# Linear attention's K^T V regrouped as (x^T K)^T Wv in a kernel with a searched instruction order

## The chip, the cores and the metric

The kernel runs on one core of a Trainium2 chip. A core has five engines that run their own instruction streams and meet at semaphores: TensorE (PE; its weight loads are shown as PEld), VectorE (DVE), ScalarE (ACT), GpSimd (POOL) and SyncE (SP), which here only issues transfers (DMAs). TensorE writes to PSUM, which DVE and ACT read; GpSimd works on SBUF alone. The metric is the time of one execution in microseconds of device time. Before the change it is 661.53 us (median of three runs, 661.41 to 661.91).

## The reference

Two attention blocks, A and B, each with an input x of 2048 rows by 512 columns in bf16, a weight wqkv of 512 by 1536 and a weight wo of 512 by 512. Both have 32 heads of 16. The outputs stand side by side, 2048 by 1024.

```python
# A: linear attention
phi = lambda t: jnp.where(t > 0, t + 1, jnp.exp(t)) + 1e-6
pq, pk = phi(q), phi(k)
kv = jnp.einsum("bhsd,bhse->bhde", pk, v)
z = jnp.einsum("bhsd->bhd", pk)
num = jnp.einsum("bhqd,bhde->bhqe", pq, kv)
den = jnp.einsum("bhqd,bhd->bhq", pq, z)[..., None] + 1e-6
o = num / den            # then o @ wo
# B: softmax attention
scores = jnp.einsum("bhqd,bhkd->bhqk", q, k) * scale
p = softmax(scores, axis=-1)
o = jnp.einsum("bhqk,bhkd->bhqd", p, v)      # then o @ wo
```

q, k and v are thirds of x @ wqkv, cut into heads.

## The kernel before

**B** is most of the work. Scores are computed transposed, in blocks of 128 keys by 512 queries, one head each: 32 heads, 16 key tiles and 4 query chunks make 2048 blocks. They are grouped into 32 units (`unit`): a group of 8 heads, a query chunk, and the even or the odd heads of the group, so that a unit has 64 blocks in four row groups of TensorE. `qk` computes a block; PV products add P times V (with a column of ones for the denominator) into `pPV`, one row group of heads to each 32 columns of TensorE.

The exponential of a block takes one of two ways:

- ACT (`fill_act_cand`): two or three blocks in `pS`, one exponential over 1024 or 1536 columns into `PT`, then one PV product for each block.
- The VectorE path (`fill_d_cand`, `d_pick`, `d_emit`): a block in a bank of `pD`, or in the third bank of `pS` (the planner's slot X), which DVE converts to an int16 that read as f16 approximates the exponential (line 980); two copies of it with other offsets, made by POOL (`on_pool`, line 1170) or by DVE (`on_dve`, line 1135); and three PV products, the first with V scaled (`VX`), the others with V (`VV`).

**A** is done in small jobs between the blocks. Each job takes one bank (`DBANK`: two of `pD` and slot X), issues its matmuls in stages and keeps the bank until a last stage has read it (`rel`). Before the change the jobs of A are, in this order:

- For each half `hp` of the 512 columns: `ak_job` and `av_job`, each eight times, for two row tiles at a time. `akv_mm` multiplies x transposed (`xTa`, loaded in chunks of 512 rows by a transposing DMA, two chunks in the buffer) by 256 columns of Wk or Wv. `ak_job` applies phi (ACT's exponential on line 686, two DVE steps on lines 687 and 689) into `KNa`; `av_job` copies to `VNa` (DVE, line 729), whose rows of 129 have a one at their end.
- `akvsum_job`, twice for each half: 16 matmuls of `KNa` tiles with 129 columns of `VNa` (line 736), then two DVE steps that mask the head blocks into `RHA` (lines 738 and 739).
- For each query chunk: `aq_job` four times (phi(q) into `PQT`), `aden_job`, and for each row tile `anum_job` and `aout_job`, the output projection and its store. `VNa` and `KNa` serve again there as `OA`, `ONT` and store buffers.

Only the first job of A's list may start, so A's jobs keep their order. Job i is not due before 40 + 560 i / N us by the planner's clock, N being the number of A's jobs: 88 before.

**The order** of every instruction on every engine is fixed when the kernel is built. A planner (the `while True` loop) keeps a clock for each engine, takes the candidate that can start first, breaks ties by priorities, and books it with a cost written in the code. A table `SEG` holds, for each stretch of the plan, 25 parameters of these choices: how many blocks go to the VectorE path at most (`RMX`, `DBL`, `PBL`), how full a batch of PV products must be (`PVQ`, `PVO`), when a shift goes to DVE (`PSH`, `DSH`), how many banks jobs may hold (`JM`), priorities, and noise with a seed (`NZ`, `SD`). The table was found by a search. Where the plan leaves PE idle, `fill_in` books products with zeros.

SP's queue issues nearly all transfers, in the order of the plan, and an issue that has to wait holds up those behind it: the loads at the start, A's x transposes (line 462), the 96 small copies that spread B's K over row groups (line 617), A's output transposes (line 795) and the stores (line 806).

Of the kernel before, what the change touches and what calls it, by code (L numbers as in the profile page):

```python
# [238 lines left out]
def bass_concat_heads__linear_attn_block__softmax_full_mha__prompt_kernel(nc, A_x, A_wqkv, A_wo, B_x, B_wqkv, B_wo, out):  # L239
# [11 lines left out]
    JM = 2  # L251
# [21 lines left out]
    DBL = 2.5  # L273
    PBL = 7.0
    SEG = (
# [66 lines left out]
    XAL = 7.0  # L342
    NZ = 0
# [16 lines left out]
    with es:  # L360
# [24 lines left out]
        VNa = sb("VNa", [128, NT, 2, 129], BF)  # L385
        PQT = sb("PQT", [128, 1, 4, 512], BF)
# [33 lines left out]
        def f32v(bk, n=512):  # L420
            return bk[0][:, bk[2]:bk[2] + n]
# [43 lines left out]
        load(Wa[:], wav, ["WaQ", "WaK"])  # L465
        wo_lane = sch.new_dma_lane()
# [48 lines left out]
        sch.add("pool", lambda e: e.memset(VNa[:, :, :, 128:129], 1.0), writes=["VNa1"])  # L515
# [177 lines left out]
        xa_left = [4] * 12  # L693
# [33 lines left out]
        def av_job(t2, hp, **kw):  # L727
            st = akv_mm(t2, hp, 2)
            st.append(("dve", 0.6, f_ev("dve", lambda e, bk: e.tensor_copy(VNa[:, t2:t2 + 2, :, 0:128], f32v(bk).rearrange("p (a b n) -> p a b n", a=2, b=2)),
                                        [], [("VNa", t2), ("VNa", t2 + 1)])))  # L730
            return Job(st, [("xA", 4 * hp + t2 // 4)] + ([("akv", hp - 1, bl) for bl in range(2)] if hp else []), [(2, ("av", hp, t2))], **kw)
# [705 lines left out]
        for hp in range(2):  # L1437
            for t in range(0, NT, 2):
                ajobs += [ak_job(t, hp), av_job(t, hp)]
# [235 lines left out]
```

## Time and profile before

| | |
|---|---|
| median of three runs | 661.53 us (661.41 to 661.91) |
| the profiled execution | 661.61 us |
| its span, first to last instruction | 659.9 us |
| granted TensorE clock, mean | 0.998 |
| score blocks in all | 2048 |
| shifts on DVE, on POOL (instructions) | 113, 369 |
| transfers on SP's queue: x transposes of A, K spreads, stores | 12, 96, 31 |
| HBM read, written | 4.46 MB, 4.19 MB |

How to read the lines that follow. A group is named by line, engine, operation and tiles, output first, with the shape of each; after the count stand the busy time, the mean duration in ns, and the idle time of the engine just before such instructions with what ended it. `x575` is the number of instructions. Instructions of one engine can overlap by a pipeline's depth, so starts can be closer than durations; matmuls do so most, and the busy time of PE counts a matmul until its modelled end. The chain of waits goes back from the last instruction to whatever released each step.

### The profile page before, as it was taken

The numbers are of one execution on the slowest core, as the hardware profiler recorded it, in microseconds if no ns is written. First come the engines' busy times: TensorE is split into PE (matmuls) and PEld (weight loads), VectorE is DVE, ScalarE is ACT, GpSimd is POOL, SyncE is SP. The second block draws the span as 40 slices with busy tenths as digits, with TensorE's granted clock in tenths as the row PEclk, the third lists the DMA queues.
The fourth block names the chain that finished last, engine by engine and source line by source line (L and its number), as shares of the span: only waits on it lengthen the run. The fifth ranks groups of instructions, "written<-read, shape, count | busy, mean of one in ns | idle before, by whom it ended". The sixth has DMA issues, their size and how long they took to land.

```text
span 659.9 us, 15950 instructions
## 1 busy us (share of the span) xinstructions
PE 633.2 (96%) x6609; PEld 200.4 (30%) x6662; DVE 632.0 (96%) x1089; ACT 644.7 (98%) x686; POOL 592.9 (90%) x450
## 2 busy tenths in 40 slices
PE   8999999999999999999999999999999999999996
PEld 5323333222333333332222233322222223232222
DVE  4999999999999999999999999999999999999994
ACT  6999999999999999999999999999999999999994
POOL 5999999999999999999998899999999999999982
PEclk9999999999999999999999999999999999999999
DMA  9701010020102101210012011010021000120002
GB/s 176 208 3 33 1 34 6 11 43 9 34 2 33 26 9 33 65 34 9 9 30 62 17 34 34 23 15 9 6 26 42 16 1 11 25 26 32 26 26 68
DMA packets 53214, 21.54 MB, mean 33 GB/s; under 512 B 44176, under 2 KB 52624, under 8 KB 53136
## 3 DMA queue, kind: packets, MB, share of 16 engines
q1 hardware_dynamic: 51664, 19.80, 13.9%
q8 instruction: 54, 0.88, 0.6%
q10 hardware_dynamic: 1472, 0.66, 0.4%
q14 instruction: 24, 0.20, 0.1%
HBM read 4.46 MB, written 4.19 MB: 13 GB/s over the span
## 4 chain that ended last, share of the span: by engine, by line
ACT 95%; PE 3%; DMA 1%; issue 0%; DVE 0%; DVEq 0%
ACT PT L1077 93%; ACT EA L686 2%; DMA xTb<-in_B_x_dram 1%; PE pPV L1247 1%; PE pD L802 1%; PE pS L864 0%; PE pD L1299 0%; PE pS L1299 0%; PE pS L1383 0%; DVE KNa L575 0%; PE pD L1383 0%; PE pD L652 0%; PE pD L864 0%; DVEq L1619 0%
## 5 line engine op out<-in xcount | busy, mean ns | idle before, releaser
L1077 ACT ACTIVATE PT<-pS 128x1024 f16<-128x1024 f32 (+1 forms) x648 | 636.6, 1305 | 1.0 <-PE pS L864 1.0
L1170 POOL TENSOR_SCALAR DI<-DI 128x2048 int16<-128x2048 int16 (+1 forms) x369 | 554.5, 1503 | 47.0 <-DVE DI L980 19.4
L980 DVE TENSOR_SCALAR DI<-pD 128x512 int16<-128x512 f32 x492 | 324.5, 679 | 6.1 <-PE pD L864 2.5
L864 PE MATMUL pS<-QT,KM 32*128 32x512 bf16 x1556 | 255.0, 384 | 8.6 <-ACT PT L1077 4.8
L1247 PE MATMUL pPV<-PT,VV 128*17 128x512 f16 x1369 | 233.7, 381 | 0.0
L1247 PE MATMUL pPV<-DI,VV 128*17 128x512 f16 x1358 | 227.3, 382 | 0.0
L864 PE MATMUL pD<-QT,KM 32*128 32x512 bf16 x492 | 170.6, 384 | 0.3 <-DVE PQT L689 0.3
L1247 PE MATMUL pPV<-DI,VX 128*17 128x512 f16 x679 | 161.0, 381 | 0.2 <-DVE OT L1276 0.2
L864 PEld LDWEIGHTS pS<-QT,KM 32*128 32x128 bf16 x1556 | 64.6, 91 | 264.8 <-ACT PT L1077 227.0
L980 DVE TENSOR_SCALAR DI<-pS 128x512 int16<-128x512 f32 x187 | 126.7, 677 | 0.7
L1135 DVE TENSOR_SCALAR DI<-DI 128x1056 int16<-128x1056 int16 x113 | 77.0, 687 | 0.5
L1247 PEld LDWEIGHTS pPV<-PT,VV 128*17 128x17 bf16 x1369 | 47.5, 88 | 41.4 <-issue 36.1
L1247 PEld LDWEIGHTS pPV<-DI,VV 128*17 128x17 bf16 x1358 | 47.0, 88 | 40.4 <-issue 33.0
L864 PEld LDWEIGHTS pD<-QT,KM 32*128 32x128 bf16 x492 | 40.6, 90 | 5.4 <-DVE DI L980 2.0
L1247 PEld LDWEIGHTS pPV<-DI,VX 128*17 128x17 bf16 x679 | 34.2, 88 | 22.0 <-issue 17.7
L711 PE MATMUL pD<-Wa,xTa 128*128 128x256 bf16 x200 | 30.5, 275 | 0.3 <-DVE DI L980 0.2
L593 PE MATMUL pD<-xTb,Wb 128*128 128x512 bf16 x67 | 21.2, 383 | 3.2 <-issue 2.3
L1276 DVE STREAM_TRANSPOSE OT<-pPV 128x512 f32<-128x512 f32 x31 | 21.9, 705 | 0.0
L575 DVE CAST KNa<-pD 128x512 bf16<-128x512 f32 x27 | 18.4, 681 | 3.0 <-PE pD L802 2.0
L1282 POOL TENSOR_TENSOR OT<-OT,ZR 128x256 bf16<-128x256 f32 x31 | 19.3, 622 | 1.6
L711 PEld LDWEIGHTS pD<-Wa,xTa 128*128 128x128 bf16 x200 | 15.5, 97 | 13.3 <-issue 6.3
L686 ACT ACTIVATE EA<-pD 128x512 bf16<-128x512 f32 x23 | 19.2, 834 | 0.0
(136 smaller groups left out, 346.0 us busy)
## 6 DMA issues: line engine op xcount, KB each, us to landing
out_dram<-KNa SPq DMA_DIRECT2D x31, 128.0 KB, 1.7
Wa<-in_A_wqkv_dram SPq DMA_DIRECT2D x1, 1536.0 KB, 7.8
KM<-KR SPq DMA_DIRECT2D x96, 16.0 KB, 1.8
Wb<-in_B_wqkv_dram SPq DMA_DIRECT2D x2, 384.0 KB, 4.3
Wb<-in_B_wqkv_dram SPq DMA_DIRECT2D x1, 512.0 KB, 5.0
Wa<-in_A_wo_dram SPq DMA_DIRECT2D x1, 512.0 KB, 4.2
Wa<-in_B_wo_dram SPq DMA_DIRECT2D x1, 512.0 KB, 4.2
ON<-in_B_x_dram ACTq DMA_DIRECT2D x1, 256.0 KB, 2.8
```

What stands on the lines that cost most here:

```text
L575: return lambda e, bk: (e.tensor_copy(out_fn(), in_fn(bk)) if lane == "dve" else e.activation(out_fn(), in_fn(bk), ACTF.Copy))
L593: return e.matmul(f32v(bk), lhsT=Wb[:, cc, kind * 512 + Gp * 128:kind * 512 + Gp * 128 + 128], rhs=xTb[:, cc, sc * 512:(sc + 1) * 512], st ...
L686: ("act", 0.052 + n * 0.000833, f_ev("act", lambda e, bk: e.activation(EA[:, 0:n], f32v(bk)[:, c0:c0 + n], ACTF.Exp), [], ["EA"])),
L711: return e.matmul(f32v(bk)[:, 256 * tt:256 * tt + 256], lhsT=xTa[:, b, cc, (o + tt) * 128:(o + tt + 1) * 128], rhs=Wa[:, cc, 512 * kind + ...
L864: return e.matmul(dst, lhsT=KM[32 * g:32 * g + 32, Gp % 2, e_, j * 128:(j + 1) * 128], rhs=QT[32 * g:32 * g + 32, Gp % 2, c * 512:(c + 1) ...
L980: sch.add("dve", lambda e: e.tensor_scalar(DI[:, buf, D0_ + i * 512:D0_ + (i + n) * 512], f32v(DBANK[b0], n * 512), ESC, EB, op0=ALU.mult, ...
L1077: sch.add("act", lambda e: e.activation(PTf[:, p0 * 512:p0 * 512 + w], S5[:, c0:c0 + w], ACTF.Exp, scale=SC), reads=skeys(sl, len(bl)), wr ...
L1135: sch.add("dve", lambda e: e.tensor_scalar(gapped(DI[:, buf, :], DIV[v], wide // 32, 32), DI[:, buf, D0_ - 32:D0_ + w], 1.0, float(SHIFT[v ...
L1170: sch.add("pool", lambda e: e.tensor_scalar(dv, sv, 1.0, sh_, op0=ALU.mult, op1=ALU.add), reads=keys, writes=[("DI", v_, x) for x, v_ in s ...
L1247: sch.add("pe", lambda e, g=g, j=j, c0=c0, V_=V_, r2=r2, P=P, first=first, last_=last_: e.matmul(PVb[32 * g:32 * g + 17, 0:512] if len(P.s ...
L1276: sch.add("dve", lambda e: e.transpose(OT[:, 0, :], PVb[:, 0:512]), reads=[("PV", g) for g in range(4)], writes=[("OT", 0)])
L1282: ("pool", 0.7, f_op("pool", lambda e: e.tensor_tensor(xn[:, :, 16 * e_:16 * e_ + 16], o[:, :, 0:16], zr.unsqueeze(2).broadcast_to([128, 1 ...
```

## The change

By the rule of matrix products phi(K)^T (x Wv) = (x^T phi(K))^T Wv. `av_job` and the projection of V are taken out. A new `axk_job` (two for each half `hp`, one for each half h of x's columns) computes x^T phi(K): 32 matmuls of 256 columns in eight stages, with x as the stationary operand in the layout it has in memory, 128 rows to a tile, and the result copied by DVE to a section of `PQT`. x's columns are loaded 256 at a time into `VNa`'s buffer, seen flat as `VNf`: the first half when the kernel starts, the second after the first `axk_job`, and the first again after the third. `akvsum_job` then has 16 matmuls of 8 columns with ones, for z, and 4 of 128 columns with Wv. `aq_job` of the first chunk waits for these sums, because `PQT` is shared. A has 76 jobs in place of 88. Chunks of x transposed are let go after two stage ends in place of four. Three base values differ (`JM`, `DBL`, and `XNL`, the planner's time for the new load) and the whole table `SEG`, 47 rows in place of 48.

```diff
-    JM = 2
+    JM = 1
-    DBL = 2.5
+    DBL = 3.0
     SEG = (
-        (0.0,0.2,4,3.0,6,1,8,3,9.5,30,2.5,3.0,0.5,2.5,2,4.0,2.0,1,1.5,2,1,0.3,4,0,0,0),
...
+        (0.0,0.3,4,3.0,6,1,8,2,9.5,30,2.0,7.0,0.8,2.5,2,4.0,2.0,2.5,0.5,1,1,-9.0,4,0,0,0),
...
     XAL = 7.0
+    XNL = 9.0
...
         VNa = sb("VNa", [128, NT, 2, 129], BF)
+        VNf = VNa[:, :, :, :].rearrange("p t b n -> p (t b n)")
...
         load(Wa[:], wav, ["WaQ", "WaK"])
+        xn_lane = sch.new_dma_lane()
+
+        def load_xn(h):
+            sch.add(xn_lane, lambda e: e.dma_start(VNf[:, 0:4096].rearrange("p (t n) -> p t n", n=256),
+                                                   A_x[0].rearrange("(t p) n -> p t n", p=128)[:, :, 256 * h:256 * h + 256]),
+                    writes=[("VNa", t) for t in range(NT)], queue="sp")
+        load_xn(0)
...
-        sch.add("pool", lambda e: e.memset(VNa[:, :, :, 128:129], 1.0), writes=["VNa1"])
+        sch.add("pool", lambda e: e.memset(VNf[:, 4096:4128], 1.0), writes=["VNa1"])
...
-        xa_left = [4] * 12
+        xa_left = [2] * 8 + [4] * 4
...
-        def av_job(t2, hp, **kw):
-            st = akv_mm(t2, hp, 2)
-            st.append(("dve", 0.6, f_ev("dve", lambda e, bk: e.tensor_copy(VNa[:, t2:t2 + 2, :, 0:128], f32v(bk).rearrange("p (a b n) -> p a b n", a=2, b=2)),
-                                        [], [("VNa", t2), ("VNa", t2 + 1)])))
...
+        def axk_job(hp, h, **kw):
+            k_ = 2 * hp + (h if hp == 0 else 1 - h)
+            sec = 2 * hp + h
+            def mm(e, bk, i):
+                x_, t = divmod(i, NT)
+                return e.matmul(f32v(bk)[:, 256 * x_:256 * x_ + 256], lhsT=VNf[:, 256 * t + 128 * x_:256 * t + 128 * x_ + 128], rhs=KNa[:, t, :],
+                                start=(t == 0), stop=(t == NT - 1))
+            st = halves(mm, [("KNa", t) for t in range(NT)] + [("VNa", t) for t in range(NT)], n=2 * NT, parts=8, dur=0.11)
+            st.append(("dve", 0.6, f_ev("dve", lambda e, bk: e.tensor_copy(PQT[:, 0, sec, :], f32v(bk)), [], [("PQT", 0, sec)])))
+            gives = [(8, ("axk", hp, h))]
+            if k_ in (0, 2):
+                st.append(("dma", XNL, lambda bk: load_xn(1 if k_ == 0 else 0)))
+                gives.append((9, ("xn", k_ + 1)))
+            return Job(st, [("ak", hp, t) for t in range(0, NT, 2)] + [("xn", k_) if k_ != 2 else ("axk", 0, 1)], gives, rel=8, **kw)
...
-            def mm(e, bk, t):
-                return e.matmul(f32v(bk, 129), lhsT=KNa[:, t, bl * 128:(bl + 1) * 128], rhs=VNa[:, t, bl, :], start=(t == 0), stop=(t == NT - 1))
-            st = halves(mm, [("KNa", t) for t in range(NT)] + [("VNa", t) for t in range(NT)] + ["VNa1"], n=16, parts=4, dur=0.085)
+            def mm(e, bk, i):
+                if i < NT:
+                    return e.matmul(f32v(bk)[:, 128:136], lhsT=KNa[:, i, bl * 128:(bl + 1) * 128], rhs=VNf[:, 4096:4104], start=(i == 0), stop=(i == NT - 1))
+                c = i - NT
+                return e.matmul(f32v(bk, 128), lhsT=PQT[:, 0, 2 * hp + c // 2, 256 * (c % 2) + 128 * bl:256 * (c % 2) + 128 * bl + 128],
+                                rhs=Wa[:, c, 1024 + 128 * bq:1024 + 128 * bq + 128], start=(c == 0), stop=(c == 3))
+            st = halves(mm, [("KNa", t) for t in range(NT)] + [("PQT", 0, 2 * hp), ("PQT", 0, 2 * hp + 1), "VNa1", "WaK"], n=20, parts=2, dur=0.04)
...
+            return Job(st, [("axk", hp, h) for h in range(2)], [(1, ("akv", hp, bl)), (3, ("rha", bq))] + ([(4, "WO")] if hp == bl == 1 else []), rel=3, **kw)
...
-            return Job(st, xn_ + [("xA", 8 + sc)] + ([("anum", sc - 1, tl) for tl in range(4)] if sc >= 1 else []),
+            return Job(st, xn_ + [("xA", 8 + sc)] + ([("anum", sc - 1, tl) for tl in range(4)] if sc >= 1 else [("akv", 1, bl) for bl in range(2)]),
...
-                ajobs += [ak_job(t, hp), av_job(t, hp)]
+                ajobs.append(ak_job(t, hp))
+            ajobs += [axk_job(hp, h) for h in ((0, 1) if hp == 0 else (1, 0))]
...
+        tok[("xn", 0)] = 36.0
```

More of the change, by code (lines that the diff above doesn't have):

```diff
@@ L725, in ak_job @@
             return Job(st, xn_ + [("xA", 4 * hp + t2 // 4)] + ([("akv", hp - 1, bl) for bl in range(2)] if hp else []), [(4, ("ak", hp, t2)), (4, ("xr", xi))], rel=4, **kw)
-        def av_job(t2, hp, **kw):
-            st = akv_mm(t2, hp, 2)
-            st.append(("dve", 0.6, f_ev("dve", lambda e, bk: e.tensor_copy(VNa[:, t2:t2 + 2, :, 0:128], f32v(bk).rearrange("p (a b n) -> p a b n", a=2, b=2)),
-                                        [], [("VNa", t2), ("VNa", t2 + 1)])))
-            return Job(st, [("xA", 4 * hp + t2 // 4)] + ([("akv", hp - 1, bl) for bl in range(2)] if hp else []), [(2, ("av", hp, t2))], **kw)
+        def axk_job(hp, h, **kw):
[12 more added lines that the diff above has]
+            return Job(st, [("ak", hp, t) for t in range(0, NT, 2)] + [("xn", k_) if k_ != 2 else ("axk", 0, 1)], gives, rel=8, **kw)
@@ L738, in akvsum_job @@
+            st = halves(mm, [("KNa", t) for t in range(NT)] + [("PQT", 0, 2 * hp), ("PQT", 0, 2 * hp + 1), "VNa1", "WaK"], n=20, parts=2, dur=0.04)
             st.append(("dve", 0.25, f_ev("dve", lambda e, bk: e.tensor_tensor(RHA[:, bq, 0:128], f32v(bk, 128), BMk[:], op=ALU.mult), ["BMk"], [("RHA", bq)])))
-            st.append(("dve", 0.15, f_ev("dve", lambda e, bk: e.tensor_tensor(
-                RHA[:, bq, 128:136], ZMk[:], bk[0][:, bk[2] + 128:bk[2] + 129].broadcast_to([128, 8]), op=ALU.mult), ["ZMk"], [("RHZ", bq)])))
+            st.append(("dve", 0.15, f_ev("dve", lambda e, bk: e.tensor_tensor(RHA[:, bq, 128:136], ZMk[:], f32v(bk)[:, 128:136], op=ALU.mult), ["ZMk"], [("RHZ", bq)])))
@@ L741, in akvsum_job @@
             if hp == bl == 1:
                 st.append(("dma", 14.0, lambda bk: load_wo()))
-            return Job(st, [(k_, hp, t) for k_ in ("ak", "av") for t in range(0, NT, 2)], [(3, ("akv", hp, bl)), (5, ("rha", bq))] + ([(6, "WO")] if hp == bl == 1 else []), rel=5, **kw)
+            return Job(st, [("axk", hp, h) for h in range(2)], [(1, ("akv", hp, bl)), (3, ("rha", bq))] + ([(4, "WO")] if hp == bl == 1 else []), rel=3, **kw)
         def aq_job(sc, bq, **kw):
```

91 rows, old and new, of the table SEG are left out of this document.

## The prediction

> **What bounds the kernel now.** I read the page's totals first, then the busy time in three stretches, then the chain of waits, then the groups of instructions by shape, and last the timeline around the steps that change.
>
> ```profile
> span 659.9 us, 15950 instructions
> PE 633.2 (96%) x6609; PEld 200.4 (30%) x6662; DVE 632.0 (96%) x1089; ACT 644.7 (98%) x686; POOL 592.9 (90%) x450
> ```
>
> The stretches (columns: width, then busy time and count of each engine):
>
> ```profile
> 0.00:40.00 40.00, 36.92 (x372) 17.18 (x379) 30.96 (x58) 33.77 (x36) 30.91 (x48) 1.00 0.73 159
> 40.00:640.00 600.00, 581.82 (x6125) 178.25 (x6164) 590.19 (x1010) 600.00 (x641) 554.28 (x392) 1.00 0.11 23
> 640.00:660.00 20.00, 14.46 (x118) 4.97 (x119) 10.89 (x23) 10.95 (x11) 7.66 (x12) 0.92 0.18 57
> ```
>
> From 40 to 640 us ACT is busy for 600.00 of 600 us. DVE has 9.8 us idle there, PE 18.2 and POOL 45.7, so ACT sets the time and two others stand close behind it. The chain says the same:
>
> ```profile
> 8.70 37.01 ACT PT L1077 x37
> ...
> 45.70 0.49 ACT EA L686
> ...
> 235.31 6.42 ACT PT L1077 x7
> ...
> 543.99 94.47 ACT PT L1077 x97
> ...
> 638.46 0.05 issue
> ```
>
> From 8.70 to 638.46 us it is ACT alone, without a gap. The time is therefore 8.7 us of start, ACT's stream, some 21 us of tail, and what lies outside the span: the profiled execution took 661.61 us, 1.7 over its span, and 0.08 over the median of 661.53. ACT's stream is exponentials of score blocks (128 keys by 512 queries), two or three to an instruction, and A's 32 exponentials at 0.49 us. Seven instructions of two blocks start 6.42 / 7 = 0.917 us apart, so **a block costs ACT 0.459 us**. The time falls only if blocks leave ACT. They can go to the VectorE path:
>
> ```profile
> L1077 ACT ACTIVATE PT<-pS 128x1024 f16<-128x1024 f32 x575 | 560.4, 1259 | 0.0
> L1170 POOL TENSOR_SCALAR DI<-DI 128x2048 int16<-128x2048 int16 x198 | 376.3, 1901 | 27.9 <-DVE DI L980 13.1 <-POOL DI L1170 2.3 <-DVE RD L763 0.2
> L980 DVE TENSOR_SCALAR DI<-pD 128x512 int16<-128x512 f32 x492 | 324.5, 679 | 6.1 <-PE pD L864 2.5 <-PE pS L864 1.2
> L1170 POOL TENSOR_SCALAR DI<-DI 128x1024 int16<-128x1024 int16 x169 | 177.0, 1047 | 18.1 <-DVE DI L980 6.3
> L980 DVE TENSOR_SCALAR DI<-pS 128x512 int16<-128x512 f32 x187 | 126.7, 677 | 0.7
> L1077 ACT ACTIVATE PT<-pS 128x1536 f16<-128x1536 f32 x73 | 121.4, 1663 | 1.0 <-PE pS L864 1.0
> L1135 DVE TENSOR_SCALAR DI<-DI 128x1056 int16<-128x1056 int16 x113 | 77.0, 687 | 0.5
> ```
>
> Of 2048 blocks 575 x 2 + 73 x 3 = 1369 are ACT's and 492 + 187 = 679 take the VectorE path. Such a block costs one conversion on DVE and two shifts. POOL makes four shifts in 1901 ns, 0.475 us each; DVE makes 113 x 2 of the 1358. It also costs PE three products with V in place of one. The timeline gives the pitch of DVE and of these products:
>
> ```profile
> 177.03 0.60 PE L1247 MATMUL pPV<-DI,VV 128*17 128x512 f16 x3
> ...
> 177.16 1.29 DVE L980 TENSOR_SCALAR DI<-pD 128x512 int16<-128x512 f32 x2
> 177.25 0.38 PE L1247 MATMUL pPV<-DI,VX 128*17 128x512 f16 x1
> ```
>
> Two conversions in 1.29 us, 0.68 each, start 0.61 us apart: neighbours overlap, so a DVE instruction of this size is worth 0.61 us, less than its 0.68. The products come in rounds of up to four, one to each column group; the rounds at 177.03 and 177.25 start some 0.216 apart, 0.054 us for a product when a round is full.
>
> **The change, part by part.** *V's projection of A goes.* Its copies and its matmuls in the trace:
>
> ```profile
> L729 DVE CAST VNa<-pD 128x512 bf16<-128x512 f32 x15 | 10.2, 683 | 0.0
> L729 DVE CAST VNa<-pS 128x512 bf16<-128x512 f32 x1 | 0.7, 681 | 0.0
> 43.33 0.61 PE L711 MATMUL pS<-Wa,xTa 128*128 128x256 bf16 x4
> 43.92 0.39 PE L864 MATMUL pS<-QT,KM 32*128 32x512 bf16 x2
> ```
>
> DVE loses 16 copies and gets 4 back, the evictions of x^T phi(K) into PQT: the same 128x512 from PSUM, so 12 x 0.61 = **7.3 us of DVE freed** (8.2 by durations). PE loses 32 stages of four 256-column matmuls and gets 32 stages of four 256-column matmuls. A stage holds it 0.59 us (43.33 to the next step at 43.92), before as after: 18.9 us each way, a difference of 0.
>
> *The sum with V becomes a sum with ones and a product with Wv.* Before, 64 matmuls of 129 columns; after, 64 of 8 columns and 16 of 128.
>
> ```profile
> L736 PE MATMUL pD<-VNa,KNa 128*128 128x129 bf16 x64 | 5.4, 222 | 0.2 <-DVE DI L980 0.2
> 177.94 0.63 PE L736 MATMUL pD<-VNa,KNa 128*128 128x129 bf16 x8
> 345.14 0.64 PE L760 MATMUL pD<-RHA,PQT 128*128 128x64 bf16 x16
> L760 PE MATMUL pD<-RHA,PQT 128*128 128x64 bf16 x64 | 2.7, 194 | 0.0
> ```
>
> Eight of 129 columns last 0.63 us with the last at 0.22: 0.059 apart. Sixteen of 64 columns: (0.64 - 0.194) / 15 = 0.030 apart. No row has 8 columns; I take 0.030, the nearest row, with 0 below and 0.059 above as bounds. New busy time: 64 x 0.030 + 16 x 0.059 = 2.9, and about 0.16 of fill (the last matmul's 0.22 less its 0.059) for each of 8 bursts, 4.2 us against 5.4: PE is freed of 1.2 us, 1.9 if a job's two stages fall together. I use 1.4; the bounds are -0.6 (0.059 each) and 3.2 (nothing each). [...]
>
> *The three loads of x* (1 MB each, half the columns, 512-byte rows) go into V's buffer from SP's queue. The nearest rows:
>
> ```profile
> Wa<-in_A_wqkv_dram SPq DMA_DIRECT2D x1, 1536.0 KB, 7.8
> KM<-KR SPq DMA_DIRECT2D x96, 16.0 KB, 1.8
> Wb<-in_B_wqkv_dram SPq DMA_DIRECT2D x1, 512.0 KB, 5.0
> 22.93 0.58 SPq L435 DMA_DIRECT2D Wa<-in_A_wqkv_dram  x1
> ```
>
> Between 5.0 and 7.8 us by size, so 6.4; the planner allows 9. The first is issued after Wa at 22.93 us and is wanted when eight K jobs are done, at 40 + 8 x 7.4, some 99 us: cost 0. The other two wait on SP for the axk matmuls that still read the buffer, and behind them queue K's spreads (wanted tens of us later), the next transposes of x and, late, the stores. In A's own order nothing follows until the load lands. That chain, two axk jobs of 8 stages at one stage per 0.92 us, a load and two short sums, is 7.4 + 6.4 + 7.4 + 4 = 25 us, and four jobs are spaced 560 / 76 x 4 = 29 us. So it fits, cost 0. Were a load 4 us later than planned, PE, which runs in order, would stand with all behind it, and ACT has one instruction, 0.9 us, in hand: some 3 us each.
>
> *The other edits* cost nothing by themselves: the ones are 32 columns as before, aq's wait for the sums stands behind them in the job list anyway, the x transposes are released after two jobs instead of four, the same 12.
>
> *What the freed time buys.* Let n blocks leave ACT; the time falls by t = 0.459 n, and every engine must finish t earlier. DVE: 7.3 = t + n x 0.61 if POOL makes all new shifts, n = 6.8 and t = 3.1; with the new shifts on DVE too (0.62 more a block) 7.3 = n x 1.69, n = 4.3 and **t = 2.0**. POOL would spend 6.8 x 0.95 + 3.1 = 9.6 of its 45.7 idle us. PE: 1.4 = t + n x 2 x 0.054 gives n = 2.5 and t = 1.1 if none of its 18.2 idle us can be used. I take t = 2.0, the lower DVE bound: it asks PE for 2.0 + 0.5 - 1.4 = 1.1 us of those 18.2. Start and tail stay. So 661.5 - 2.0 = **659.5 us**, with 658.4 to 660.4 by these bounds; with the sums at their dear end, -0.6, and no idle time of PE used, t is -0.5 and the time 662.0.
>
> **The rivals.** *The new order finds more* (0.20). Speaking for it: 45.7 us of POOL idle beside 113 shifts on DVE. Twelve of these on POOL cost it 11.4 us and give DVE another 7.3. PE then decides: if it yields 3.5 of its idle us, t = (3.5 + 1.4) x 0.459 / 0.567 = 4.0, 657.5 us. Against: these idle us were there before, and 19.4 of POOL's are waits for a conversion:
>
> ```profile
> POOL DI L1170 <- DVE DI L980: 19.4, 51, 1.0
> PEld pS L864 <- ACT PT L1077: 227.0, 522, 0.7
> ```
>
> *PE is the real bound and DVE was never short* (0.18). Then 7.3 us of DVE merely become idle, PE's 1.4 us are lost in its many handoffs, and the blocks stay about 679: 661.3 us. For it: PE at 97.0% and its 522 weight loads behind ACT, each one slot early or late. Against: DVE is fuller, 98.4%.
>
> *Slower: the bank held by axk* (0.20). Three PSUM banks serve conversions and jobs (two of pD, one of pS, which took 187 of 679). An axk job keeps one over 8 stages and its eviction, some 8 us, four times: 32 us, in which 1.13 conversions per us, 36, want a place. If a third of these find none, 12 blocks go to ACT instead of 4 leaving it, as far as the order does not make up for it; it decides from 4 lost blocks up, and seven is 0.2% slower. With ten lost, (10 - 4.3) x 0.459 = 2.6, 664 us. Against: the 16 V jobs held a bank for 16 x (1.8 + 0.7) = 40 us, though in short pieces.
>
> **How the numbers follow.** The forecast has 0.42, the rivals 0.20, 0.18 and 0.20. A measurement of this kernel tells from no change about 0.2%, 1.3 us. The forecast's upper end lies just within that, so a little of it goes to no change; the rival without an effect spreads to both sides. Faster 0.58, same 0.20, slower 0.22. The range takes in the larger gain with room below it and most of the slower case: 656.0 to 663.8.
>
> **What would show it.** Right: the VectorE path takes 682 to 686 conversions and ACT 1362 to 1366 blocks; no V copies and four evictions into PQT; DVE's idle between 40 and 640 us again near 10 us; ACT without a gap until some 636.5 us. Matmuls of 8 columns 0.030 apart. The bank rival shows as fewer than 679 conversions and conversions bunched outside the axk jobs; the PE rival as DVE idle grown by 7 us with as many conversions; the larger gain as fewer than 113 shifts on DVE and 688 or more conversions. A PE gap of over 1 us that a load of x ends, with ACT idle behind it, would prove the load's price of 0 wrong. A tail longer than some 21 us after ACT's stream would break the sum by itself.

## The result, and the profile after

The changed kernel takes **664.08 us** (median of seven runs, 663.25 to 664.54) against 661.62 (661.41 to 661.91) for the kernel before: a ratio of 1.0036, 95% interval 1.0026 to 1.0046. It is slower by 2.5 us, where 659.5 was forecast. The profiled execution took 664.19 us. The page's totals after, then the stretches (width, then busy time and count of PE, PEld, DVE, ACT, POOL):

```profile
span 661.0 us, 15972 instructions
PE 633.5 (96%) x6626; PEld 201.8 (31%) x6680; DVE 624.5 (94%) x1076; ACT 644.9 (98%) x684; POOL 592.9 (90%) x437
```

```profile
40.00:640.00 600.00, 581.32 (x6121) 179.29 (x6165) 580.87 (x991) 599.61 (x640) 555.60 (x382) 1.00 0.12 27
```

DVE lost 7.5 us of work (632.0 to 624.5), as it should. But between 40 and 640 us its idle time went from 9.8 to 19.1 us: what was freed was not used. The groups by shape say the same:

```profile
L1093 ACT ACTIVATE PT<-pS 128x1024 f16<-128x1024 f32 x570 | 554.5, 1241 | 0.1
L996 DVE TENSOR_SCALAR DI<-pD 128x512 int16<-128x512 f32 x495 | 327.2, 679 | 14.0 <-PE pD L880 9.2 <-PE pS L880 2.3
L996 DVE TENSOR_SCALAR DI<-pS 128x512 int16<-128x512 f32 x185 | 125.2, 677 | 0.8 <-PE pS L880 0.6
L1093 ACT ACTIVATE PT<-pS 128x1536 f16<-128x1536 f32 x76 | 123.7, 1627 | 1.3 <-PE pS L880 1.0 <-PE pD L880 0.2
```

ACT has 570 x 2 + 76 x 3 = 1368 blocks, DVE 495 + 185 = 680: **one block moved**, not four. The wait of the conversions in `pD` for PE's scores, 2.5 us in ten waits before, is 9.2.

ACT still looks busy for 599.61 of 600 us, but that hides waits: its instruction of two blocks lasts 1.24 us and the next one starts 0.92 us after it, so a delay of up to some 0.3 us leaves no gap. The chain of waits shows them. Between 117 and 171 us it leaves ACT where it had not before, and again between 225 and 252 (start, length, what):

```profile
8.53 35.18 ACT PT L1093 x35
...
117.19 0.93 ACT PT L1093
...
124.60 1.01 PE pD L736 x8
125.93 0.98 PE pD L736 x8
127.23 0.54 PE pD L736 x4
128.10 0.54 PE pD L736 x4
129.17 0.99 PE pD L736 x8
130.19 0.69 DVE PQT L739
...
168.47 0.98 PE pD L736 x8
169.77 0.98 PE pD L736 x8
171.12 15.61 ACT PT L1093 x16
```

L736 is now axk. A stage of four matmuls holds PE 0.54 us and two in a row 0.98, while the order books a stage at 4 x 0.11 = 0.44. The excess of 0.10 comes once each time PE takes up axk, not once for each matmul. The timeline there:

```profile
125.54 0.39 PE L880 MATMUL pS<-QT,KM 32*128 32x512 bf16 x2
...
125.86 1.05 PE L736 MATMUL pD<-KNa,VNa 128*128 128x256 bf16 x8
...
126.84 0.39 PE L880 MATMUL pS<-QT,KM 32*128 32x512 bf16 x2
```

ACT's next scores come 1.30 us after the last ones (125.54 to 126.84), where its instructions of two blocks otherwise start 0.92 apart: it waits.

The end, in the timeline of before and then of after:

```profile
647.15 2.60 ACT L1077 ACTIVATE PT<-pS 128x1024 f16<-128x1024 f32 x2
...
652.12 0.40 POOL L1339 TENSOR_TENSOR OT<-OT,ZR 128x128 bf16<-128x128 f32 x1 [0.64 <-DVE ZR L1338]
...
652.56 0.69 DVE L575 CAST KNa<-pD 128x512 bf16<-128x512 f32 x1 [0.52 <-PE pD L802]
...
653.16 0.43 DVE L1342 STREAM_TRANSPOSE xTb<-OT 128x256 bf16<-128x256 bf16 x1
...
655.20 0.68 DVE L575 CAST KNa<-pS 128x512 bf16<-128x512 f32 x1
```

```profile
648.41 1.71 ACT L1093 ACTIVATE PT<-pS 128x1536 f16<-128x1536 f32 x1
...
652.66 0.40 POOL L1355 TENSOR_TENSOR OT<-OT,ZR 128x128 bf16<-128x128 f32 x1 [0.64 <-DVE ZR L1354]
...
653.95 0.69 DVE L579 CAST KNa<-pD 128x512 bf16<-128x512 f32 x1 [1.37 <-PE pD L1315]
...
654.56 0.43 DVE L1358 STREAM_TRANSPOSE xTb<-OT 128x256 bf16<-128x256 bf16 x1
655.05 0.60 PE L1315 MATMUL pS<-Wa,xTb 128*128 128x512 bf16 x2 [0.27 <-DVE xTb L1358]
...
655.70 0.69 DVE L579 CAST KNa<-pS 128x512 bf16<-128x512 f32 x1 [0.70 <-PE pS L1315]
```

After the change, the last transposition could start when POOL is done at 653.06; it stands on DVE behind a cast that waits 1.37 us for PE, and starts at 654.56, 1.5 us late. Before, POOL was done at 652.52, the cast ahead waited 0.52 us, and the transposition was 0.64 us late. The stores' time from issue to landing, before and after:

```profile
DMA to landing us min/median/max: 1.7/2.7/2.8
```

```profile
DMA to landing us min/median/max: 1.7/2.6/3.4
```

The two profiled executions, put side by side from these records (us from the span's start):

| | before | after | later by |
|---|---|---|---|
| end of ACT's last block | 649.75 | 650.13 | 0.38 |
| last store issued | 655.91 | 656.41 | 0.12 more |
| last store landed | 658.72 | 659.85 | 0.63 more |
| end of the span | 659.88 | 661.01 | 0 more |
| time of the execution | 661.61 | 664.19 | 1.45 more |

ACT started 0.17 us earlier (8.53) and had one block, 0.46 us, less to do; it should have ended 0.63 earlier and ended 0.38 later, so some 1.0 us went in its waits. The last row holds the time outside the span. It was 1.7 to 1.9 us in every run of before and 2.5 to 3.2, mean 2.9, in the seven of after: 1.1 us of the 2.5 lie where no row of the profile shows anything.

### The profile page after: what moved, and what is told of

The parts are those of the page before. It is cut to its first block, busy times and chain, and to the rows that moved or that the text cites. A ratio compares the mean times of both kernels' runs of the same rounds, so it can differ in the third digit from the quotient of the medians.

```text
span 661.0 us, 15972 instructions
## 1 busy us (share of the span) xinstructions
PE 633.5 (96%) x6626; PEld 201.8 (31%) x6680; DVE 624.5 (94%) x1076; ACT 644.9 (98%) x684; POOL 592.9 (90%) x437
## 4 chain that ended last, share of the span: by engine, by line
ACT 85%; PE 11%; DVE 2%; DMA 1%; issue 0%; DVEq 0%
ACT PT L1093 82%; PE pS L880 3%; PE pPV L1263 3%; PE pD L736 2%; ACT EA L690 2%; DVE DI L996 2%; DMA xTb<-in_B_x_dram 1%; PE pD L597 1%; PE pD L880 0%; PE pS L1315 0%; PE pD L1315 0%; DVE DI L1151 0%; PE pS L1399 0%; DVE PQT L739 0%; DVE OT L1292 0%
## 5 line engine op out<-in xcount | busy, mean ns | idle before, releaser
L1263 PE MATMUL pPV<-DI,VV 128*17 128x512 f16 x1360 | 230.4, 382 | 0.0
L996 DVE TENSOR_SCALAR DI<-pS 128x512 int16<-128x512 f32 x185 | 125.2, 677 | 0.8 <-PE pS L880 0.6
L1151 DVE TENSOR_SCALAR DI<-DI 128x1056 int16<-128x1056 int16 x107 | 73.2, 687 | 0.6
L597 PE MATMUL pD<-xTb,Wb 128*128 128x512 bf16 x92 | 28.7, 383 | 3.9 <-issue 2.4
L736 PE MATMUL pD<-KNa,VNa 128*128 128x256 bf16 x128 | 18.0, 274 | 0.0
L674 PE MATMUL pD<-Wb,xTb 128*128 128x128 bf16 x224 | 17.2, 220 | 0.3
L818 PE MATMUL pD<-Wa,KNa 128*128 128x512 bf16 x46 | 14.7, 383 | 1.7 <-issue 1.5
```

Of the source, the lines that this page charges most:

```text
L597: return e.matmul(f32v(bk), lhsT=Wb[:, cc, kind * 512 + Gp * 128:kind * 512 + Gp * 128 + 128], rhs=xTb[:, cc, sc * 512:(sc + 1) * 512], st ...
L674: return e.matmul(f32v(bk)[:, tl * 128:(tl + 1) * 128], lhsT=xTb[:, cc, t * 128:(t + 1) * 128], rhs=Wb[:, cc, 1024 + Gp * 128:1024 + Gp * ...
L736: return e.matmul(f32v(bk)[:, 256 * x_:256 * x_ + 256], lhsT=VNf[:, 256 * t + 128 * x_:256 * t + 128 * x_ + 128], rhs=KNa[:, t, :], start= ...
L996: sch.add("dve", lambda e: e.tensor_scalar(DI[:, buf, D0_ + i * 512:D0_ + (i + n) * 512], f32v(DBANK[b0], n * 512), ESC, EB, op0=ALU.mult, ...
L1151: sch.add("dve", lambda e: e.tensor_scalar(gapped(DI[:, buf, :], DIV[v], wide // 32, 32), DI[:, buf, D0_ - 32:D0_ + w], 1.0, float(SHIFT[v ...
L1263: sch.add("pe", lambda e, g=g, j=j, c0=c0, V_=V_, r2=r2, P=P, first=first, last_=last_: e.matmul(PVb[32 * g:32 * g + 17, 0:512] if len(P.s ...
```

## The experiments

Times are medians; "before" ran beside each set on the same chip, at 661.59 to 661.83. The sets ran on different chips, so a comparison across sets is looser than one within. Span and outside are means over the runs. The last three columns are from the profiled execution: conversions, ACT's stream from the start of its first score block to the end of its last, and the tail from there to the end of the span.

| run | time | span | outside | conversions | ACT's stream | tail |
|---|---|---|---|---|---|---|
| before, first set | 661.78 | 660.06 | 1.78 | 679 | 641.06 | 10.13 |
| after | 664.08 | 661.13 | 2.92 | 680 | 641.60 | 10.88 |
| e1_axk_192 | 662.89 | 659.96 | 2.94 | 680 | 640.42 | 11.06 |
| e2_after_old_table | 674.92 | 673.20 | 1.77 | 669 | 652.25 | 11.60 |
| e3_before_new_table | 677.08 | 675.08 | 1.98 | 670 | 652.14 | 13.41 |
| e4_one_lane | 664.22 | 661.27 | 2.96 | 680 | 641.62 | 11.04 |
| p1_after_pad64 | 662.94 | 661.17 | 1.77 | 680 | 641.61 | 11.03 |
| p2_after_pad160 | 662.96 | 661.27 | 1.77 | 680 | 641.61 | 11.37 |
| p3_before_pad160 | 661.89 | 660.16 | 1.74 | 679 | 641.05 | 10.48 |
| s1_before_searched | 661.82 | 660.12 | 1.78 | 681 | 640.20 | 11.31 |
| s2_after_searched | 662.29 | 660.37 | 1.79 | 677 | 643.03 | 9.18 |
| s3_dve_relief | 662.03 | 660.34 | 1.74 | 682 | 641.03 | 11.14 |
| s4_pe_relief | 662.13 | 660.30 | 1.76 | 682 | 639.69 | 12.18 |
| s5_both_relief | 660.90 | 659.26 | 1.76 | 684 | 639.55 | 10.86 |
| f1_before_searched_tail | 661.13 | 659.38 | 1.74 | 681 | 640.20 | 10.47 |
| f2_after_tail | 662.37 | 660.50 | 1.76 | 680 | 641.61 | 10.20 |
| t1_pe_wait | 665.32 | 663.52 | 1.81 | 680 | 641.61 | 13.21 |

ACT's stream repeats closely: the six profiles of the changed kernel's order (after, e4, p1, p2, f2, t1) have 641.60 to 641.62.

**The stages of axk, booked too short.** The order is left as it is; each axk matmul takes 192 of 256 columns, so that a stage really takes about what the order booked (in its trace four matmuls hold PE 0.44 us); 64 of K's 256 columns are left out of A's sums.

```diff
-                return e.matmul(f32v(bk)[:, 256 * x_:256 * x_ + 256], lhsT=..., rhs=KNa[:, t, :],
+                return e.matmul(f32v(bk)[:, 256 * x_:256 * x_ + 192], lhsT=..., rhs=KNa[:, t, 0:192],
```

> The changed kernel with its order kept, instruction for instruction; each axk matmul multiplies 192 of the 256 columns, so x^T phi(K) is left incomplete. Theory short booking: an axk stage of four 256-column matmuls holds TensorE 0.54 to 0.58 us and is booked in the plan at 0.44; two such stages together stretch ScalarE's pitch from 0.92 to 1.3 us, some 2 us in all around 125, 132, 170, 233 and 251 us. With 192 columns a stage holds it about 0.46 us: those stretches vanish and the time falls by 1.0 to 2.0 us, to 662.1 to 663.1. Rival, the order as a whole (too few blocks moved) or what lies outside the span: 663.8 to 664.4, no change.

The chain of e1 between 117 and 171 us, two pieces in place of the many above:

```profile
116.96 0.49 ACT EA L690
117.45 54.26 ACT PT L1093 x55
```

The chain stays on ACT there and between 225 and 252 us too. ACT's stream is 1.2 us shorter, and the time falls to 662.89, from 664.08 (664.22 for e4 in the same set). So the short booking costs about 1.2 us in this order. That is the price of 32 x 0.10 = 3.2 us of PE that the order didn't count; an order that counts them has to find them elsewhere (s2 below). The conversions stay at 680, their order being fixed.

**The dataflow and the table exchanged.** In one kernel the table `SEG` of before stands in the changed kernel, in the other that of after stands in the kernel before.

```diff
     SEG = (
-        (0.0,0.3,4,3.0,6,1,8,2,9.5,30,2.0,7.0,0.8,2.5,2,4.0,2.0,2.5,0.5,1,1,-9.0,4,0,0,0),
+        (0.0,0.2,4,3.0,6,1,8,3,9.5,30,2.5,3.0,0.5,2.5,2,4.0,2.0,1,1.5,2,1,0.3,4,0,0,0),
...
```

> The changed dataflow with the table (SEG, JM, DBL) of the kernel before, so the planner makes another order. Theory, a table fits only the dataflow it was searched on: 8 to 16 us slower than before, 670 to 678, with some ten conversions fewer on the VectorE path. Rival, the dataflow is worth 2 us by itself and the new table lost it: 658 to 661.

> The dataflow of before with the new table. Theory, a table fits only its dataflow: 670 to 678. Rival, the new table is a weaker table as such and the dataflow does not matter: 663 to 666.

Both lose some 13 to 15 us (ratios 1.0199, 1.0182 to 1.0216; 1.0230, 1.0213 to 1.0247), with some ten conversions fewer, as expected. A table fits only the dataflow that it was searched for, so such an exchange can't say what the dataflow is worth. The runs s1 to s5 were searched for that reason.

**The semaphore of the new loads.** The time outside the span is longer after; the changed kernel has one DMA semaphore more. Here the loads of x use that of the loads of wo.

```diff
-        xn_lane = sch.new_dma_lane()
+        xn_lane = wo_lane = sch.new_dma_lane()
...
-        wo_lane = sch.new_dma_lane()
```

> The changed kernel with the x loads on the semaphore of the output weights' loads, so as many DMA semaphores as before; every engine's order stays. The profiled execution of the change lies 3.2 us over its span, that of before 1.7. Theory, that comes with the order of the tail or from run to run: 663.8 to 664.4. Rival, the one more semaphore costs it: 662.4 to 662.9.

664.22 us, 2.96 outside: the semaphore is not it.

**Where the program's end lies.** Waits that are never reached are put into the branch that serves large scores and is not taken; all that stands behind it moves on in each engine's stream.

```diff
             with e.If(got[0] > THRESHOLD_BITS):
...
                 gsch.emit_queue(queue, e, gsems)
+                for _ in range(64):                # 160 in p2 and p3
+                    e.wait_ge(sems[flag_op.lane], flag_op.count)
```

> The changed kernel with 64 more waits for the flag on each engine inside the branch for large scores, which is never taken: nothing more is executed, but what stands behind the branch in each engine's instruction stream lies 64 instructions further on. In the runs so far the time outside the span was 1.7 to 1.9 us for the kernel before and 2.2 to 3.8 us (mean about 2.9) for the changed one. Theory: this 1.1 us is where the program's last instructions happen to lie in the stream (they are fetched anew). Then the padding moves it: outside the span some 1.8 us and a time near 663.0, or another value than 2.9 in any case. Rival: it belongs to the changed work (its loads, its stores); then the padding changes nothing, 2.9 us outside and 664.1.

> As the run with 64 waits, with 160. Theory: a second position, so a second value of the time outside the span, between 1.7 and 3.8 us, that can differ from both others; time 663.0 to 664.1. Rival: 2.9 us outside the span and 664.1, whatever the number.

> The kernel before with 160 more waits inside the branch that is never taken. Theory (position of the last instructions): the time outside the span can leave its 1.8 us, up to some 2.9, with the span still 659.9: 661.7 to 662.9. Rival (the changed work): 1.8 us outside as ever, 661.7.

With 64 or with 160 waits the changed kernel has 1.77 us outside its span like every other, in all 20 runs, and takes 662.94 and 662.96 us (ratios 1.0020, 1.0010 to 1.0029; 1.0024, 1.0014 to 1.0033). It isn't the changed work as such: e2 and s2 do the same work by other orders, without the waits, and have 1.77 and 1.79. So **1.1 us of the loss depends on where the changed program's last instructions lie**, as far as these runs tell; the changed kernel without the waits was not run on the chip of p1 and p2, so a part of that chip in it isn't excluded. Other positions did nothing: the kernel before stayed at 1.74 with 160 waits, where up to 2.9 had been thought possible, and 160 gave the changed kernel no second value. What happens in that time no run shows.

**What freed time buys.** The order was searched anew by one method, with the effort of the control or less, for the kernel before (s1, the control), for the changed kernel with axk and the short sums booked at what they take (s2), for the kernel before with some 6.4 us less of DVE (s3: 16 copies of 282 ns in place of 682), with some 7 us less of PE (s4), and with both (s5).

```diff
# s2
-            st = halves(mm, ..., n=2 * NT, parts=8, dur=0.11)
+            st = halves(mm, ..., n=2 * NT, parts=8, dur=0.14)
-            st = halves(mm, ..., n=20, parts=2, dur=0.04)
+            st = halves(mm, ..., n=20, parts=2, dur=0.045)
# s3, s5
-            st.append(("dve", 0.6, ... e.tensor_copy(VNa[:, t2:t2 + 2, :, 0:128], f32v(bk)...
+            st.append(("dve", 0.2, ... e.tensor_copy(VNa[:, t2:t2 + 2, :, 0:32], f32v(bk)...[:, :, :, 0:32])
-                return e.matmul(f32v(bk, 129), ..., rhs=VNa[:, t, bl, :], ...
+                return e.matmul(f32v(bk, 129), ..., rhs=KNa[:, t, 0:129], ...
# s4, s5: for V alone
+            if kind == 2:
...                                                  # mm2: as mm, with cc in 0, 1
+                return chunked(halves(mm2, ["WaK", ("xA", b)], n=4, parts=2, dur=0.16), 4 * hp + t2 // 4)
```

> The kernel before with another table of the order, from a new search of ours over the same parameters; nothing else is changed. It is the control for the next three, whose tables come from the same search with the same or less effort. The table places 681 conversions on DVE against 679 (2 blocks less on ACT, 0.9 us by 0.459 us a block). If the order of before left something to find: 660.5 to 661.2. If the search has found only what the chip does not keep (waits that it books too short, a tail that lands later): 661.5 to 662.5. Both theories on DVE and PE are indifferent to it.

> The changed kernel with a stage of axk booked at 0.56 us of PE instead of 0.44 (the trace has 0.54), the short sums at 0.045 a matmul instead of 0.04, and a table searched anew for it with the same effort as the control. Theory (the change frees DVE, but PE has to take part in every block that moves, and the gain that the published order counts on lay in PE time booked too short): no faster than the control, 0.5 to 2 us slower, 661.5 to 663.0, with some 677 conversions, and without the stretches of ACT at the axk steps. Rival (the dataflow is worth its 2 us and only the order spoilt it): 1.5 to 2.5 us faster than the control, 659 to 660.

> The kernel before with DVE relieved alone: each of A's 16 V copies takes 128 of the 512 columns, booked at 0.2 us instead of 0.6, some 0.45 us less each, 7 us in all, as much as the change frees; the sums read K in V's place, in the same sizes, so A's output is another. PE, ACT and POOL do the same work. Table searched anew. Theory (PE is in the way of blocks that move): within 0.7 us of the control. Rival (the prediction's: DVE limits): 7.0 / 7.3 x 2.0, some 1.9 us below the control, with 4 conversions more.

> The kernel before with PE relieved alone: A's V products take two of the four steps of the contraction, two matmuls a stage instead of four, 0.32 us instead of 0.54, 32 x 0.22 = 7 us in all; A's output is another. DVE, ACT and POOL do the same work. Table searched anew. Theory (PE is in the way): 1 to 2 us below the control, as the pieces of PE between ACT's handoffs come free. Rival (DVE limits): within 0.5 us of the control. If both this and the run with DVE relieved fall by some 0.5 to 1 us, neither engine alone sets the time, and each holds a part.

> The kernel before with both reliefs at once: A's V copies take 128 of 512 columns (7 us of DVE) and A's V products two of four steps (7 us of PE); the sums read K in V's place; A's output is another. Table searched anew; it places 684 conversions, against 681 of the control and 682 of each relief alone. Theory (DVE and PE both have to take part in each block that moves, so that relief of one alone buys nothing): the stream of ACT ends 1.5 to 2 us earlier than in either single relief, and the time is 660.0 to 660.8. Rival (the gain is lost in ACT's short waits and the tail, whatever engine is relieved): 661.5 to 662.3, as the single reliefs.

The control is level with before: ratio 1.0002 (0.9993 to 1.0012). Its stream of ACT is 0.9 us shorter and its tail takes that back. The changed kernel with honest costs is at 1.0006 (0.9996 to 1.0015), with 677 conversions: this dataflow brings no gain that can be measured, as the theory put down for s2 said. It is level only by its tail, 2.1 us shorter than the control's; its stream is 2.8 us longer.

By the time, relief of DVE alone gives nothing (1.0004, 0.9995 to 1.0014), as the theory put down for s3 said; but relief of PE alone gives nothing either (1.0003, 0.9993 to 1.0012), where it had expected 1 to 2 us. That expectation was wrong. Both together give 0.9986 (0.9977 to 0.9996): 684 conversions and 660.90 us, 0.9 below the control and 1.1 to 1.2 below either alone, just outside the 660.0 to 660.8 that was expected.

That a block needs DVE and PE at the same time to leave ACT would fit these times, but they don't show it. The stream was to end 1.5 to 2 us earlier with both reliefs than with either alone. It is 1.5 us shorter than with DVE's, but only 0.1 shorter than with PE's; what s5 gains on s4 lies in the tail (10.86 against 12.18). And each kernel has one table of one search: s3, which has less work than the control and nothing more, came out with a stream 0.8 us longer. Differences of that size in the streams of s1, s3, s4 and s5 can be the search's, and those of some tenths between their times mean nothing.

**The tail.** The second of the last four evictions goes to ACT in place of DVE, so that it can't stand ahead of the last transposition: in the control's order (f1) and in the changed kernel with the 64 waits (f2).

```diff
-                    lane = "dve" if tl in (1, 3) else "act"
+                    lane = "dve" if tl == 3 else "act"
```

> The control (kernel before, table of our search) with ACT in place of DVE for the second of the four last evictions of B's output. In the control this eviction stands on DVE ahead of the last transposition (653.56), which was ready at 652.4 when POOL was done and starts only after it. Theory (this order in the tail gave back what the stream gained: ACT's last block there ends at 648.81 against 649.75 before, its tail is 11.31 against 10.13): the last store is issued some 0.8 us earlier, 654.6, and the time is 660.9 to 661.2, under both kernels. Rival (the last stores land no earlier, whatever their issue): 661.8 as the control.

> The changed kernel with its own table, 64 waits in the branch that is never taken, and the same edit of the tail. Theory: the last store is issued at some 655.6 in place of 656.4, and the time is 662.94 less 0.8, 662.0 to 662.4. Rival: 662.9 as with the waits alone.

The timeline of the control s1, then that of f1:

```profile
651.98 0.40 POOL L1344 TENSOR_TENSOR OT<-OT,ZR 128x128 bf16<-128x128 f32 x1 [0.64 <-DVE ZR L1343]
...
652.95 0.69 DVE L580 CAST KNa<-pD 128x512 bf16<-128x512 f32 x1 [1.05 <-PE pD L1304]
...
653.56 0.43 DVE L1347 STREAM_TRANSPOSE xTb<-OT 128x256 bf16<-128x256 bf16 x1
```

```profile
652.10 0.40 POOL L1344 TENSOR_TENSOR OT<-OT,ZR 128x128 bf16<-128x128 f32 x1 [0.64 <-DVE ZR L1343]
...
652.54 0.45 DVE L1347 STREAM_TRANSPOSE xTb<-OT 128x256 bf16<-128x256 bf16 x1 [0.51 <-POOL OT L1344]
```

The transposition now follows POOL directly, 1.02 us earlier; the last store is issued at 654.87 in place of 655.42, less than the 0.8 us expected, because that cast and the third are now ACT's in a row. f1 takes **661.13 us**, 0.9990 of before (0.9981 to 1.0000), a gain at the edge of what the interval tells. f2 takes 662.37, 0.6 below p1, which ran in another set; against the kernel before beside each it gains 0.8, as expected.

**The landing of the last stores.** In the changed kernel with the 64 waits PE waits for the stores before it takes its last branch.

```diff
+            if queue == "pe":
+                for s_ in stores[-4:]:
+                    e.wait_ge(sems[s_.lane], 16 * s_.count)
             with e.If(got[0] > THRESHOLD_BITS):
```

> The changed kernel with 64 waits in the branch that is never taken, and with PE waiting for the last four stores to land before it branches over that code; PE's branch takes 3.8 us in the changed kernel (655.86 to 659.63), in which instructions are fetched, and the last two stores land in 3.4 us where the two before them land in 1.7 to 1.8. Theory (this fetch of PE is what holds the stores): they land in 1.7 to 2.5 us, while PE's branch ends only some 3.5 us after them, so that the span grows by about 1 us. Rival (the fetches of the other engines or the stores themselves): they land in 3.4 us as before, and the span grows by some 3 us.

The stores' view of t1:

```profile
DMA to landing us min/median/max: 1.7/1.8/2.8
```

ACT's store lands in 1.80 us and SP's last in 2.79, where both took 3.6 in p1 and 3.4 in the changed kernel's trace. So it is PE's branch that holds ACT's store, and a part of what holds SP's last one: it lasts 3.8 us in the changed kernel's trace (655.86 to 659.63), four packets of the instruction queues fall in it (three of q14, one of q8), and the stores issued meanwhile land later. What keeps the last one above 1.8 was not taken apart; DVE, ACT and SP branch then too (0.05 to 0.07 us each in that trace). It is no gain: the branch now runs from 659.49 to 663.12, and the span grows by 2.4 us, where about 1 was expected.

## Why the prediction was wrong

- **ACT sets the time**: right as the bound, but after the change it waits within its 599.61 busy us, as the chain shows.
- **DVE freed of 7.3 us**: right. The copies of 10.2 + 0.7 us are gone and four evictions of 686 ns came, 8.2 us less by durations, as reckoned. That DVE's whole busy time fell by 7.5 is a near agreement by chance, as it also holds six long shifts fewer, four short ones and one conversion more.
- **The sums**: right (2.7 + 1.5 = 4.2 us by the groups of L750 and L752), from a row that the trace of before didn't have:

```profile
177.21 0.56 PE L750 MATMUL pD<-VNa,KNa 128*128 128x8 bf16 x16
```

```profile
L750 PE MATMUL pD<-VNa,KNa x64: 166/166/180, 177.2 to 264.3; 128*128 128x8 bf16 x64
```

  The first row is the timeline's, the second the view of this line. Sixteen in 0.56, the last in 0.166: 0.026 us apart, against 0.030 taken.
- **The loads of x cost nothing**: right.

```profile
VNa<-in_A_x_dram SPq DMA_DIRECT2D x3, 1024.0 KB, 5.7
```

  The two loads within the stream took 5.7 us, where 6.4 was taken; the one at the start took 10.6, long before it was wanted. No PE step waits for one.
- **"A difference of 0" for 32 stages against 32**: right on the chip, 0.54 us each for axk and for K's projection. But the order booked axk at 0.44, 32 x 0.10 = 3.2 us of PE that don't exist, and ran into them. This lay in the diff beside the row of 0.59 us, and I didn't compare the two. It cost 1.2 us (e1).
- **"I take t = 2.0 ... it asks PE for 1.1 us of those 18.2"**: this is the step that failed. One block moved, not 4.3, and with axk booked at what it takes (s2) none did: 677 conversions and a time level with before. The idle time of PE that I leaned on was partly an artefact of the profile. p3 carries out the steps of the kernel before and p1 those of the changed kernel, and from 40 to 640 us their rows have every matmul (p3, then p1):

```profile
40.00:640.00 600.00, 589.59 (x6176) 178.30 (x6168) 590.22 (x1009) 600.00 (x641) 554.23 (x392) 1.00 0.11 23
```

```profile
40.00:640.00 600.00, 589.62 (x6172) 179.17 (x6164) 580.88 (x992) 599.61 (x640) 554.77 (x382) 1.00 0.12 27
```

  The row of before has 6125 matmuls to 6164 weight loads: 51 of p3's 6176 are missing there, and with them 7.8 us of busy time. PE had 10.4 idle us and not 18.2, as few as DVE with 9.8, and it has 10.4 again after the change, while DVE's doubled. My other bound, t = 1.1 "if none of its 18.2 idle us can be used", was nearer, and still above what either relief alone gave. The formula treated each engine's idle time as one sum that moved blocks can draw on. In s3 and s4 some 7 us freed on one engine bought no time; with both freed the time fell by 0.9 us, as far as one searched table each can tell. Which waits keep a block from moving stays open.
- **"Start and tail stay"**: wrong, by nearly as much as the gain that was forecast: 0.75 us from ACT's last block to the end of the span (0.12 of order, 0.63 of landing), and 1.1 outside it.
- **The rivals.** "PE is the real bound and DVE was never short" gave the right mark, DVE's idle time grown by 9.3 us with as many conversions (680), and the wrong time, 661.3, as it had neither the booking, the tail nor the end. Its cause is neither shown nor ruled out: relief of PE alone took 0.5 us off ACT's stream, within the search's scatter, and nothing off the time. The slower rival's 664 us is right by chance: the bank that axk holds was to show as fewer than 679 conversions, and there are 680. No larger gain: DVE's shift instructions fell from 113 to 111 (107 long, four short), conversions hardly rose.

Taken together: 664.08 less 1.2 (booking) less 1.1 (the end's place) is 661.8, level with the kernel before; this is added up, no run has both. The tail's edit would bring some 0.6 to 0.8 more (f2), but it brought the control 0.7 as well (f1), so it says nothing on the dataflow. What stays open is what the program does in the 1.1 us outside the span, and what kept s5 from the 2 us that its five blocks more than before, 5 x 0.459 = 2.3, would be worth: ACT's stream is 1.5 us shorter there, and the tail takes 0.7 longer than before.

## What to carry to other kernels

Where several engines stand within some per cent of the bound, price a moved piece of work by what it needs on all of them; the idle time of each, added up over the span, is no budget, and for PE compare matmul records with weight loads before trusting it. A bounding engine whose instructions overlap can wait without an idle gap (ACT's of two blocks last 1.24 us here and start 0.92 apart): read the chain of waits, and the distance between starts. Compare every cost that a planned order books with a row of the profile, above all the new ones: what is booked too short comes back as waits on the bounding engine (1.2 us here, by e1). Differences of 1 us in 660 can come from the last ten microseconds (0.75 us here) and from where the program's end lies (1.1 us); look at the stream of the bounding engine, the tail and the time outside the span separately before crediting a dataflow. Where the order is searched, one table for each variant leaves the scatter of the search in the comparison.

## What had not been expected of the hardware

- With the program's last instructions 64 or 160 places further on, the time outside the span was 1.77 us in place of 2.9 in one kernel (on another chip), and the same as ever in the other (1.74). With 160, the steps from the last landing to the end of the span took 1.49 us in place of 1.16, in both kernels.
- PE's branch over the code for large scores took 3.4 to 4.1 us in the profiled executions (3.45 before, 3.77 after). Nearly all stores issued meanwhile landed in 2.7 to 3.9 us, and those issued just before it in 1.7 to 1.8; with PE held back (t1) one landed in 1.80 and one in 2.79.
- A stage of four 256-column matmuls between other work held PE 0.54 us, 0.10 longer than its 4 x 0.11; two in a row held it 0.98, 0.10 longer as well.
- A matmul of 8 columns started 0.026 us after the one before (sixteen in 0.56 us).
